# One level of Strassen's algorithm in the spatial product of a four-layer attention and gMLP kernel

## The chip, the cores and the metric

The kernel runs on one core of a Trainium2 chip. The metric is the device time of one execution in microseconds (us). The time before is the median of three runs.

## The reference

The input x has 2048 rows of 640 values. Four sublayers are added to it in turn: A, B, A, B, with the same weights in both rounds ("layer 1" and "layer 2" below; the code counts them 0 and 1).

A is an attention with memory: x is normalised, multiplied by wq, wk and wv, and treated in 4 segments of 512 rows and 32 heads of 20 columns. Each segment has a softmax attention within itself and a read from a memory matrix that the earlier segments have filled. The result goes through wo.

B is a gated product with mixing along the rows, and it is the part that the change touches:

```python
def _B_ref(x, w_in, w_sp, b_sp, w_out):
    z = _gelu(jnp.einsum("bsd,df->bsf", x, w_in))        # 640 -> 1728
    z1 = z[..., :Fh]                                     # Fh = 864
    z2 = _layernorm(z[..., Fh:], axis=-1)
    g = jnp.einsum("ts,bsf->btf", w_sp, z2) + b_sp[None, :, None]
    return jnp.einsum("bsf,fd->bsd", z1 * g, w_out)
```

The product of w_sp (2048 x 2048) with z2 (2048 x 864) is called the spatial product here.

## The kernel before, in words

The rows of x stand in 16 tiles of 128. All large products are made in 16-bit floats with a correction: each operand is split into a high and a low part (h, l), and three matmuls (h x h, h x l, l x h) take the place of one. Splitting takes one ScalarE operation (the scaled high part) and one VectorE operation (the rest). Where an operand must be turned, one DMA transpose from SBUF to SBUF turns both parts. All DMAs are issued from SyncE (SP), in one queue.

A layer has three stages, which follow one another in the code and overlap at their ends.

- **Attention (phase1a, L1195).** For each segment: normalised rows are split and turned into xt0 or xt1 (`prep`, L667), value products are made tile by tile (`value`, L686), query and key products in units of 128 columns (`unit`, L742), then logits, exponentials and their products with the values. The order of the matmuls is written out by hand: `run` (L1034) gives each piece of work a due time in steps, and streams named fills, background, dense and reads are merged by these times. `early` (L1041) does the first four tiles' rows and values and the first unit before the steps begin. The last results of a segment are cast and stored as ohl (L1022), in the same buffers (tag xh) that `prep` uses for its split rows. The weights wv, wq and wk are split once, in layer 1, and stay in SBUF for both layers (L177, L183).
- **phase1b (L302).** For each of the 16 tiles: the attention's output product (only tiles 12 to 15, the others had it in phase1a; `attn_out`, L331), normalisation of the row tile (xn), its split and transpose (`xn_t`: xnhl, then th), two half products with w_in of 30 matmuls of 432 columns each (`w_in_half`, L356), and the gelu. The second half gives z2: it is normalised and split into zh and zl, which stay in SBUF for all 16 tiles (`z2_half`, L367). The first half gives z1, which is stored (`z1_half`, L374). The weights of the second half (wi1) and wo are loaded during attention, those of the first half (wi0) near its end (L312).
- **phase2 (L400).** For each of the 16 tiles t: `rows(t)` loads 128 rows of w_sp, takes each row's largest value (L427), makes a power of two of it, splits the scaled rows in two halves of 1024 columns (L437, L438) and turns each half by a DMA transpose into wt (L439). `spatial(t)` makes 16 x 3 x 2 = 96 matmuls of 432 columns into one accumulator gp (L450), copies it with scale and bias (L453), multiplies with z1 (L455), takes the largest value of each row (L457), splits (L463, L464) and turns (L466) the result u into ut. `tail(t)` makes the output product with w_out, 42 matmuls (L479), adds x and stores the row tile (L482, L483). The loop issues spatial(t), rows(t+1), tail(t-1).

Buffers belong to pools; pools are laid out in SBUF one after another in the order in which they are opened, from the left end or (side="right") from the right end, and a stage's pools take over the addresses of the stage before. A new buffer waits only for the buffers of the old stage whose addresses it covers. Two padding tiles named gap (L309 in phase1b, 1945 words; L406 in phase2, 5580 words a partition) set which addresses meet. The order of the instructions on each engine other than the hand-written one is chosen when the kernel is built, by priority (the order in the code, raised by `high_priority`) and by when a modelled operand is ready.

## Time and profile before

| what | us |
|---|---|
| median of three runs | 2308.09 (2307.16 to 2308.31) |
| the profiled execution's own time | 2313.21 |
| its span from the first to the last instruction | 2311.5 |
| PE busy | 2167.8 |
| VectorE busy | 1372.8 |
| ScalarE busy | 1139.0 |
| GpSimd busy | 987.0 |

One execution of the kernel was recorded. In the profile, PE is TensorE's matmuls and PEld its weight loads, DVE is VectorE, ACT ScalarE, POOL GpSimd, SPq the queue of SyncE that issues the DMAs. A line such as `L450 PE MATMUL gp<-zh,wt` names the line of the kernel, the engine, the operation, the tile written and the tiles read; after it stand the shapes, the count, the busy time and the mean duration in ns, and then the idle time of the engine ahead of these instructions and what ended it. In a timeline the first number is the start in us, the second the length in us, and the brackets tell how long the engine had been idle and what ended that. The chain of waits follows the work that ended last back to the beginning; its lines give start, length, and what the time went to. The stages lie in the span as follows: attention to 613 us, phase1b to 813, phase2 to 1187, attention of layer 2 to 1731, phase1b to 1934, phase2 to the end; neighbouring stages overlap.

### The profile page before, as it was taken

The page shows a single profiled execution, that of the slowest core. Times are in us where ns is not written, and L with a number is a line of the kernel's source. Part 1 is how long each engine was busy: PE and PEld are TensorE (multiplying, and loading weights), DVE is VectorE, ACT ScalarE, POOL GpSimd, SP SyncE. Part 2 cuts the span into 40 slices and gives each one's busy share as a digit, 9 for nine tenths or more (in the row PEclk, how much of TensorE's full clock was granted, in tenths as well). Part 3 has the DMA queues.
Part 4 walks back from the last instruction along what each step waited for, and adds up shares of the span by engine and source line. Part 5 has one row for each costly group of instructions (what it writes and reads, how often), then busy time and mean ns, then how long its engine had stood idle before and what let it go on. Part 6 is the DMA issues. An engine that isn't in the chain of part 4 may idle for free.

```text
span 2311.5 us, 52604 instructions
## 1 busy us (share of the span) xinstructions
PE 2167.8 (94%) x21706; PEld 1306.2 (57%) x21706; DVE 1372.8 (59%) x2577; ACT 1139.0 (49%) x1344; POOL 987.0 (43%) x976
## 2 busy tenths in 40 slices
PE   5888889999899999999998989999989999999998
PEld 3455555666555555555554556566665555555554
DVE  7678878777754544343327786777756443534331
ACT  3578788888532322121126987888863322212110
POOL 2387889999610000000104988899991100000000
PEclk9999999999899999999999999999999999999999
DMA  5566665345743687566634465443565347756561
GB/s 167 148 159 157 169 165 133 84 119 133 212 127 86 150 231 158 160 156 162 148 86 107 113 149 144 124 102 106 139 172 127 94 118 201 164 155 163 154 147 47
DMA packets 512113, 325.60 MB, mean 141 GB/s; under 512 B 411488, under 2 KB 454368, under 8 KB 507520
## 3 DMA queue, kind: packets, MB, share of 16 engines
q1 hardware_dynamic: 511872, 322.23, 54.5%
q8 instruction: 170, 2.79, 0.5%
q14 instruction: 71, 0.58, 0.1%
HBM read 148.46 MB, written 85.61 MB: 101 GB/s over the span
## 4 chain that ended last, share of the span: by engine, by line
PE 56%; DMA 4%; POOL 4%; DVE 3%; ACT 3%; issue 2%; SPq 1%; DVEq 0%; ACTq 0%; POOLq 0%
PE gp L450 23%; PE zp L363 13%; PE cyp L479 8%; POOL PL L970 3%; PE qps L756 2%; PE pv L998 2%; PE vps L697 2%; PE kps L756 1%; PE mp L895 1%; DMA th<-xnhl 1%; PE yps L729 1%; PE yp L340 1%; ACT P L933 1%; PE es L895 1%; DVE mxs L959 1%
## 5 line engine op out<-in xcount | busy, mean ns | idle before, releaser
L970 POOL TENSOR_TENSOR PL<-P,PH 128x640 f16<-128x640 f32 x380 | 535.5, 1434 | 53.3 <-PE pv L998 43.6
L450 PE MATMUL gp<-zh,wt 128*128 128x432 f16 x2048 | 462.3, 346 | 0.0
L450 PEld LDWEIGHTS <-wt 128*128 128x128 f16 x3072 | 300.5, 98 | 257.6
L959 DVE TENSOR_REDUCE mxs<-mp 128x2 f32<-128x1024 f32 (+2 forms) x384 | 320.0, 861 | 140.5 <-PE mp L886 139.0
L933 ACT ACTIVATE P<-es,sc 128x1024 f32<-128x1024 f32 (+1 forms) x256 | 271.5, 1060 | 99.1 <-PE es L886 84.9
L465 POOL MEMSET un<- 128x64 f16 x32 | 5.0, 155 | 665.9 <-DMA ut<-un 632.7
L363 PEld LDWEIGHTS <-th 128*128 128x128 f16 x1920 | 188.6, 99 | 173.5 <-DMA th<-xnhl 9.7
L450 PE MATMUL gp<-zl,wt 128*128 128x432 f16 x1024 | 270.6, 346 | 0.0
L453 ACT ACTIVATE u<-gp,bsp,un 128x864 f32<-128x864 f32 x32 | 34.2, 1070 | 431.1 <-PE gp L450 419.6
L968 ACT CAST PH<-P 128x1280 f16<-128x1280 f32 x192 | 239.7, 1248 | 1.6
L272 POOL TENSOR_TENSOR lnrs<-lnve,mhalf 128x1 f32<-128x1 f32 x96 | 60.2, 635 | 421.2 <-DVE lnve L271 374.5
L427 DVE TENSOR_REDUCE am<-wr 128x1 f32<-128x2048 f32 x32 | 73.1, 2286 | 210.2 <-DMA wr<-in_B_w_sp_dram 210.2
L970 POOL TENSOR_TENSOR PL<-Pb,PH 128x640 f16<-128x640 f32 x124 | 177.1, 1454 | 12.4 <-PE pv L998 8.0
L697 PE MATMUL vps<-wvh,xt 128*128 128x320 f16 x640 | 156.6, 313 | 25.5 <-DVE relu L788 19.6
L479 PE MATMUL cyp<-wuh,ut 128*128 128x320 f16 (+1 forms) x896 | 165.1, 301 | 5.8 <-DMA ut<-un 5.8
L895 PEld LDWEIGHTS <-qk 64*128 64x128 f16 (+1 forms) x2048 | 78.2, 94 | 160.4 <-issue 140.0
L479 PEld LDWEIGHTS <-ut 128*128 128x128 f16 (+1 forms) x1344 | 132.1, 98 | 61.6 <-DMA ut<-un 6.6
L998 PE MATMUL pv<-vs,PL 128*128 128x41 f16 x2560 | 157.0, 181 | 4.7 <-POOL PL L970 4.3
L998 PE MATMUL pv<-vs,PH 128*128 128x41 f16 x2560 | 159.5, 182 | 1.1 <-DVE ab L1014 0.8
L363 PE MATMUL zp<-wi1h,th 128*128 128x432 f16 x640 | 151.2, 352 | 7.8 <-DMA th<-xnhl 7.6
L895 PE MATMUL es<-qk 64*128 64x512 f16 (+3 forms) x1024 | 124.8, 300 | 27.7 <-ACT P L933 20.1
L363 PE MATMUL zp<-wi0h,th 128*128 128x432 f16 x640 | 148.3, 346 | 0.0
(189 smaller groups left out, 4294.5 us busy)
## 6 DMA issues: line engine op xcount, KB each, us to landing
wr<-in_B_w_sp_dram SPq DMA_DIRECT2D x32, 1024.0 KB
qk<-st SPq DMA_DIRECT2D x256, 120.0 KB
z<-z SPq DMA_DIRECT2D x32, 432.0 KB
cz<-z SPq DMA_DIRECT2D x32, 432.0 KB
xt<-in_A_x_dram SPq DMA_DIRECT2D x32, 320.0 KB
st<-qhl SPq DMA_DIRECT2D x40, 256.0 KB
st<-khl SPq DMA_DIRECT2D x40, 256.0 KB
x<-x SPq DMA_DIRECT2D x32, 320.0 KB
```

What stands on the lines that cost most here:

```text
L363: nc.tensor.matmul(zp[:, n, :FHH], a[:, k, :], b[:, k, c:c + FHH], start=(k == 0 and j == 0), stop=(k == KD - 1 and j == 2))
L427: nc.vector.tensor_reduce(am, wr, AX.X, ALU.max, apply_absolute_value=True)
L450: nc.tensor.matmul(gp[:, n, :FHH], wt[:, k // 8, a, k % 8, :], b[:, k, n * FHH:(n + 1) * FHH], start=(k == 0 and j == 0), stop=(k == NT - ...
L479: nc.tensor.matmul(yp[:, n, :320], a[:kn[k], k, :], b[:kn[k], k, n * 320:(n + 1) * 320], start=(k == 0 and j == 0), stop=(k == KO - 1 and ...
L697: nc.tensor.matmul(ps, a[:, k, c], b[:, k, n * 320:(n + 1) * 320], start=(i == 0), stop=(i == 14))
L756: nc.tensor.matmul(ps, a[:, k, c], b[:, k, :], start=(i == 0), stop=(i == 14))
L895: nc.tensor.matmul(out[:, h, o:o + w], a[r, ac], b[r, bc], start=o == 0, stop=False, skip_group_check=True)
L933: g.exp = nc.scalar.activation(P, E, AF.Exp, scale=g.esc)
L959: e = nc.vector.tensor_reduce(mx[:, :, n, j], mp[:, :, o:o + w], AX.X, ALU.max)
L968: nc.scalar.copy(PH, P[:, h])
L970: (nc.gpsimd if h == 0 or n < self.N - self.TAIL else nc.vector).tensor_tensor(PL[:, c], P[:, h, c], PH[:, c], ALU.subtract)
L998: nc.tensor.matmul(pv[:, i, h, :], x[:, c:c + 128], v[:, j, h0 + h, :], start=(j == 0 and x is PH), stop=(j == i and x is PL), skip_group_ ...
```

## The change

The 16 tiles are paired as t and t + 8; the rows and columns of w_sp, and the rows and columns of z2, are thus cut into two halves each, so that the spatial product is a product of 2 x 2 blocks. It is made by one level of Strassen's algorithm (Winograd's form: four sums or differences of blocks for each operand): seven block products in place of eight.

- **phase1b** takes the tiles in the order 0, 8, 1, 9, ... and makes of each pair's z2 seven blocks of 432 columns (b11, b21, b22 of z2 itself, and four differences made on GpSimd), each split into zh and zl by ScalarE and VectorE. zh and zl grow from 16 x 864 to 8 x 7 x 432 columns each, 96.8 KB a partition in place of 55.3. The staging of w_in's first half uses the buffers of w_sp's rows. The padding goes.
- **phase2** works in 8 pairs. `rows(p)` loads both tiles' rows in two column parts, makes the same kind of sums and differences on w_sp (two on GpSimd, two on VectorE for each part), and splits and turns 14 blocks of 512 columns, into 17 buffers. The two tiles of a pair have scales of their own; their ratio, a power of two, enters the differences. The scales are kept from layer 1 for layer 2. `pair(p)` makes seven products of 8 x 3 matmuls of 432 columns into three accumulators, which ScalarE and VectorE read in between, and places the two tails of the pair before after the second and the fifth product. `finish` is the part of `spatial` after the copy.
- The query and key weights no longer stay in SBUF. In layer 1 they are stored to DRAM by 20 DMAs from the background stream of phase1a, at step 45, and in layer 2 they are loaded again by 4 DMAs. Their room is used by w_sp's rows and their split parts, and the start of zh, in phase1b and phase2. The pools for wo and wi1 change places.

The core of the diff:

```diff
-ZS = 1024.0
+ZS = 256.0
+WSP = 4096.0
...
-        for nm in "vqk":
-            g.w[nm] = [wp.tile([128, KD, D], F16, name=f"w{nm}{x}") for x in "hl"]
+        g.w["v"] = [wp.tile([128, KD, D], F16, name=f"wv{x}") for x in "hl"]
+        g.wqk = {nm + x: nc.dram_tensor(f"w_{nm}{x}", (128, KD, D), F16, kind="Internal").ap() for nm in "qk" for x in "hl"}
...
-        p2, p1, px1, gap = pool("b2", 2), pool("b1", 1), pool("bx1", 1), pool("bgap", 1)
+        p2, p3, px1 = pool("b2", 2), pool("b1", 3), pool("bx1", 1)
...
-        wi0 = g.wi[0].load(sp)
+        wi0 = g.wi[0].load(g.prep[0], 864, "wr")
...
+        def block(k, j, src):
+            nc.scalar.copy(zh[:, k, j, :], src)
+            nc.vector.tensor_tensor(zl[:, k, j, :], src, zh[:, k, j, :], ALU.subtract)
...
+            if t < 8:
+                b11, b12 = z[:, :FHH], z[:, FHH:]
+                block(k, 0, b11)
+                sub(b11, b12, b11)
+                block(k, 4, b11)
+                return
+            t1, b12 = z2[k][:, :FHH], z2[k][:, FHH:]
+            b21, b22 = z[:, :FHH], z[:, FHH:]
+            sub(t1, b22, t1)
+            block(k, 1, b21)
+            sub(b12, b12, b22)
+            block(k, 2, t1)
+            sub(b21, b21, t1)
+            block(k, 3, b12)
+            block(k, 5, b22)
+            block(k, 6, b21)
...
+WB = ("11", "12", "s2", "s3", "s1", "s4", "22")
...
+        def rows(p):
+            ws = []
+            for c in range(2):
+                w = pr.tile([128, S], F32, tag="wr", name="wr").rearrange("p (r h c) -> p r h c", r=2, h=2)
+                for r in range(2):
+                    t = p + 8 * r
+                    nc.sync.dma_start(w[:, r], w_sp[t * 128:(t + 1) * 128, :].rearrange("p (h c) -> p h c", h=2)[:, :, c * 512:(c + 1) * 512])
+                ws.append(w)
+            if not g.wsp_scaled:
...
+                def part(nm, src, r):
+                    hl = ph.tile([128, 2, 512], F16, tag="wn", name="wn")
+                    nc.scalar.activation(hl[:, 0], src, AF.Identity, scale=iv[r])
+                    nc.vector.scalar_tensor_tensor(hl[:, 1], src, iv[r], hl[:, 0], ALU.mult, ALU.subtract)
+                    t = blocks[nm, c] = pt.tile([128, 2, 4, 128], F16, tag="wt", name="wt")
+                    nc.sync.dma_start(t.rearrange("p l k c -> p (l k) c"), hl.rearrange("p l c -> p (l c)"), transpose=True)
+
+                part("11", a11, 0)
+                part("22", a22, 1)
+                nc.gpsimd.tensor_tensor(a22, a21, a22, ALU.add)
+                nc.vector.scalar_tensor_tensor(a21, a21, rho, a11, ALU.mult, ALU.subtract)
+                nc.vector.scalar_tensor_tensor(a11, a22, rho, a11, ALU.mult, ALU.subtract)
+                part("12", a12, 0)
+                part("s2", a11, 0)
+                nc.gpsimd.tensor_tensor(a12, a12, a11, ALU.subtract)
+                part("s3", a21, 0)
+                part("s1", a22, 1)
+                part("s4", a12, 0)
...
+        def product(ps, blocks, j, start):
+            for k in range(NP):
+                wt = blocks[WB[j], k // 4]
+                for i, (a, z) in enumerate(((0, zh), (0, zl), (1, zh))):
+                    nc.tensor.matmul(ps, wt[:, a, k % 4, :], z[:, k, ZB[j], :], start=start and k == 0 and i == 0,
+                                     stop=k == NP - 1 and i == 2, skip_group_check=True)
...
-            ut = p1.tile([128, 2, KO, 128], F16, tag="ut", name="ut")
+            ut = p2.tile([128, 2, KO, 128], F16, tag="ut", name="ut")
...
+            A = bank("ga")
+            product(A, blocks, 0, True)
+            copy(0, left)
+            C = bank("gc")
+            product(C, blocks, 1, True)
+            add(0, left, C)
+            if pend:
+                tail(*pend[0])
+            product(A, blocks, 2, False)
+            copy(1, left)
+            B = bank("gb")
+            product(B, blocks, 3, True)
+            product(A, blocks, 4, False)
+            copy(1, right)
+            add(1, right, B)
+            if pend:
+                tail(*pend[1])
+            product(A, blocks, 5, False)
+            copy(0, right)
+            f0 = finish(p, u[0])
+            product(B, blocks, 6, False)
+            add(1, left, B)
+            return f0, finish(p + 8, u[1])
...
+            if not g.wo.made:
+                for i, (nm, x, k) in enumerate((nm, x, k) for nm in "qk" for x in range(2) for k in range(KD)):
+                    with self.tc.issue_after(self.fetched.ins):
+                        self.nc.sync.dma_start(g.wqk[nm + "hl"[x]][:, k], g.w[nm][x][:, k])
+                    yield 45 + .05 * i
...
+                with tc.tile_pool(name="wqk", bufs=1, reuse_waits="tile") as qp:
+                    for nm in "qk":
+                        g.w[nm] = [qp.tile([128, KD, D], F16, name=f"w{nm}{x}") for x in "hl"]
+                        for hl, t in zip("hl", g.w[nm]):
+                            if layer:
+                                nc.sync.dma_start(t, g.wqk[nm + hl])
+                    phase1a(g, x, o_d, x1_d)
+                g.prep = [zs.enter_context(tc.tile_pool(name=n, bufs=b, reuse_waits="tile")) for n, b in (("cr", 2), ("ch", 3))]
...
-                zh = zp.tile([128, NT, FH], F16, name="zh")
-                zl = zp.tile([128, NT, FH], F16, name="zl")
+                zh = zp.tile([128, NT // 2, 7, FHH], F16, name="zh")
+                zl = zp.tile([128, NT // 2, 7, FHH], F16, name="zl")
```

More of the change, by code (lines that the diff above doesn't have):

```diff
@@ L302, in phase1b @@
 def phase1b(g, o_d, x, x1_d, z1_d, zh, zl):
+    ORDER = [t + 8 * r for t in range(NT // 2) for r in range(2)]
     nc, tc = g.nc, g.tc
@@ L447, in spatial @@
-            for k in range(NT):
-                for j, (a, b) in enumerate(((0, zh), (0, zl), (1, zh))):
-                    for n in range(2):
-                        nc.tensor.matmul(gp[:, n, :FHH], wt[:, k // 8, a, k % 8, :], b[:, k, n * FHH:(n + 1) * FHH],
-                                         start=(k == 0 and j == 0), stop=(k == NT - 1 and j == 2))
-            u = p1.tile([128, FH], F32, tag="u", name="u")
-            nc.scalar.activation(u.rearrange("p (n c) -> p n c", n=2), gp[:, :, :FHH], AF.Identity,
-                                 bias=bsp[:, t:t + 1], scale=un)
@@ L483, in tail, with pair, copy, add @@
             nc.sync.dma_start(out[t], xo.rearrange("p n c -> p (n c)"))
+        def pair(p, blocks, pend):
+            bank = lambda nm: pg.tile([128, 512], F32, tag=nm, name=nm)[:, :FHH]
+            un = [sc[:, 2, p, r:r + 1] for r in range(2)]
+            bias = [bsp[:, p + 8 * r:p + 8 * r + 1] for r in range(2)]
+            u = [p1.tile([128, FH], F32, tag=f"u{r}", name="u") for r in range(2)]
+            left, right = slice(0, FHH), slice(FHH, FH)
+            def copy(r, c):
+                nc.scalar.activation(u[r][:, c], A, AF.Identity, bias=bias[r], scale=un[r])
+            def add(r, c, ps):
+                nc.vector.scalar_tensor_tensor(u[r][:, c], ps, un[r], u[r][:, c], ALU.mult, ALU.add)
+            A = bank("ga")
[21 more added lines that the diff above has]
+            return f0, finish(p + 8, u[1])
         with tc.high_priority(offset=HP):
-            wt = rows(0)
-        wu = g.wu.load(sp, D)
+            blocks = rows(0)
+        wu = g.wu.load(p2, D, "xo")
         for _ in range(g.wu.nk + 1):
@@ L490, in phase2 @@
         pend = None
-        for t in range(NT):
-            if t == 5:
+        for p in range(NP):
+            if p == 2:
                 g.wu.keep()
-            u = spatial(t, wt)
-            wt = rows(t + 1) if t + 1 < NT else None
-            if pend is not None:
-                tail(*pend)
-            pend = (t, *u)
-        tail(*pend)
+            f = pair(p, blocks, pend)
+            blocks = rows(p + 1) if p + 1 < NP else None
+            pend = f
+        g.wsp_scaled = True
+        for f in pend:
+            tail(*f)
 def consts(g, ctx):
@@ L516, in consts @@
     g.sc = cp.tile([128, 11], F32, tag="sc", name="sc")
+    g.wsc = cp.tile([128, 4, NT // 2, 2], F32, tag="wsc", name="wsc")
+    g.wsp_scaled = False
     g.wap = cp.tile([128, 4, 10], F32, tag="wap", name="wap")
```

98 lines of the change are left out of this document (50 added, 48 removed).

## The prediction, made before the changed kernel was run

> **What bounds the kernel now.** I read the page's busy times first, then the busy times of each engine by stage (columns: stretch, its length, then busy us and instructions of PE, PEld, DVE, ACT, POOL, then granted clock, DMA share, GB/s), then the chain of waits.
>
> ```profile
> PE 2167.8 (94%) x21706; PEld 1306.2 (57%) x21706; DVE 1372.8 (59%) x2577; ACT 1139.0 (49%) x1344; POOL 987.0 (43%) x976
> 840.00:1175.00 335.00, 334.03 (x1992) 194.56 (x1991) 142.23 (x259) 60.82 (x59) 13.94 (x28) 1.00 0.64 159
> 1930.00:2290.00 360.00, 360.00 (x2127) 207.84 (x2125) 138.79 (x239) 61.66 (x58) 2.42 (x16) 1.00 0.61 152
> 1012.45 17.52 PE gp L450 x96
> 1029.97 5.71 PE cyp L479 x42
> ```
>
> The second and third lines are the two spatial stages (phase2): the matmul engine is busy for the whole stretch at full clock, everything else at most 64%. The chain is there nothing but 17.52 us of spatial product and 5.71 us of output product, tile after tile: 23.23 us a tile, 46.46 us for the two tiles t and t+8. So a matmul taken out of this stage comes out of the time, until another thing is late.
>
> **What is removed.** 96 matmuls of 432 columns take 17.52 us: 0.1825 us each. A pair of tiles takes 192 of them now; seven products of 8 x 3 are 168. One product is 24 x 0.1825 = 4.38 us, and one product fewer for 8 pairs in 2 layers is 16 x 4.38 = 70.1 us. Every matmul already has its own weight load (21706 of each), so smaller products add none. A pair should take 7 x 4.38 + 2 x 5.71 = 42.1 us.
>
> **What has to fit into 42.1 us.** The other engines' costs, by kind:
>
> ```profile
> L437 ACT ACTIVATE wn<-wr,ivw 128x1024 f16<-128x1024 f32 x64 | 73.0, 1147 | 128.4 <-DMA wt<-wn 112.3 <-DVE ivw L432 16.0
> L438 DVE SCALAR_TENSOR_TENSOR wn<-wr,ivw,wn 128x1024 f16<-128x1024 f32 x64 | 81.7, 1279 | 49.8 <-ACT wn L437 49.7
> L427 DVE TENSOR_REDUCE am<-wr 128x1 f32<-128x2048 f32 x32 | 73.1, 2286 | 210.2 <-DMA wr<-in_B_w_sp_dram 210.2
> L774 DVE SCALAR_TENSOR_TENSOR khl<-kps,khl 128x512 f16<-128x512 f32 x40 | 27.2, 681 | 13.7 <-ACT relu L773 13.7
> L794 DVE SCALAR_TENSOR_TENSOR phl<-relu,sc,phl 128x512 f16<-128x512 f32 x30 | 37.1, 1236 | 7.7 <-ACT phl L793 7.7
> L285 POOL TENSOR_TENSOR xnhl<-xt,xnhl 128x640 f16<-128x640 f32 x32 | 44.7, 1401 | 95.1 <-ACT xnhl L284 94.9
> 1006.70:1029.90 23.20, 23.20 (x140) 13.49 (x138) 10.02 (x17) 4.27 (x4) 0.15 (x1) 1.00 0.62 158
> ```
>
> VectorE now spends 10.0 us a tile (last line), 20.0 a pair, of which the four splits are 5.1 and the two reductions 4.6. The change makes 14 splits of 512 columns (0.68 each, L774's 681 ns: 9.5), four more such operations for the differences (2.7), three additions out of PSUM (some 0.6 each, an estimate from the same row: 1.8) and drops nothing else: 20.0 - 5.1 + 9.5 + 2.7 + 1.8 = 29 us of 42.1 in layer 1. In layer 2 the scales are kept, which takes off the 4.6: 24. ScalarE goes from 8.5 to some 12 by halves of L437's 1.15. GpSimd gets four operations of 512 columns, at most 1.4 us each by the 640-column row. None is the bound by its sum.
>
> DMA: 0.62 of 23.2 us is 14.4 us a tile, 28.8 a pair. The transposes grow from four of 512 KB to fourteen of 256 KB.
>
> ```profile
> 1030.00 4.65 SPq L439 DMA_TRANSPOSE wt<-wn  x2
> 1034.50 1.15 ACT L437 ACTIVATE wn<-wr,ivw 128x1024 f16<-128x1024 f32 x1 [3.42 <-DMA wt<-wn]
> 1036.77 1.15 ACT L437 ACTIVATE wn<-wr,ivw 128x1024 f16<-128x1024 f32 x1 [0.21 <-DMA wt<-wn]
> ```
>
> Two transposes go out at 1030.00; their buffers come free at 1034.50 and 1036.77, so the second costs 2.27 us. Fourteen halves are 15.9 us where four wholes were 9.1: 28.8 + 6.8 = 35.6 us of 42.1, 85%. That fits: of 17 wt buffers three are free for the next pair at once, each half product (2.2 us) leaves another, and a block is used about a pair later. I take nothing for it; it costs something when DMA takes over 1.18 times this price.
>
> **The output product of a pair's first tile.** Its u is complete only after the sixth product; its tail comes after the second product of the next pair, 3 x 4.38 = 13.1 us later. Now it has a whole tile.
>
> ```profile
> 1053.24 1.07 ACT L453 ACTIVATE u<-gp,bsp,un 128x864 f32<-128x864 f32 x1 [15.32 <-PE gp L450]
> 1061.41 1.30 SPq L466 DMA_TRANSPOSE ut<-un  x1
> 1066.65 0.15 POOL L465 MEMSET un<- 128x64 f16 x1 [24.25 <-DMA ut<-un]
> 2288.66 0.43 PE L479 MATMUL cyp<-wuh,ut 128*128 128x320 f16 x2
> 2299.37 0.71 PE L479 MATMUL cyp<-wuh,ut 128*128 128x320 f16 x2 [4.84 <-DMA ut<-un]
> 2299.37 8.03 PE cyp L479 x42
> ```
>
> From the end of a tile's products to the landing of its transpose: 13.4 us amid other work (1053.24 to 1066.65), 10.7 us at the end of the kernel, where nothing else runs (2288.66 to 2299.37). The new copy is half as wide (0.5 us less). So 10.2 to 12.9 against 13.1, with busier queues: a wait of 0 to 3 us for each of the 14 pairs that have a pair before them. I take 0.4 us, near the lower end because the sum still closes: **6 us** (0 to 41).
>
> **From layer 1's phase2 to layer 2's attention.** Until now padding tiles keep layer 2's first buffers (xt0, the x rows) off phase2's late ones, and the value products fill the waits:
>
> ```profile
> 1169.18 0.43 PE L479 MATMUL cyp<-wuh,ut 128*128 128x320 f16 x2
> 1174.89 0.30 PE L697 MATMUL vps<-wvh,xt 128*128 128x320 f16 x1
> 1181.17 5.71 PE cyp L479 x42
> 1196.90 0.59 PE L756 MATMUL qps<-xt,wqh 128*128 128x512 f16 x2
> ```
>
> 27.7 us from the last spatial matmul (1169.18) to the first query product, all full. The change takes the padding for the wider zh and zl. By the pools' sizes in order (per partition from the end of the value weights: 25.6 KB of query/key weights, then attention's pools) xt0 lies at 137 to 147 KB and the x rows at 147 to 152, where phase2 then has ut, x1 and w_out at 135 to 172. The first x row can be loaded only after the last tail's matmuls. Then: first tail at 10.2 - 4.4 = 5.9 us after the last product, 8.0 long at a half clock (2299.37 row), second tail 5.7: 19.6. Then load, statistics, scaling, split, transpose:
>
> ```profile
> 1735.68 2.78 DMA o<-ohl
> L269 DVE BATCH_NORM_STATS2 lnst<-xt 128x6 f32<-128x320 f32 x64 | 28.1, 477 | 13.7 <-DMA xt<-x 12.1 <-DMA xt<-in_A_x_dram 1.6
> L680 DVE TENSOR_SCALAR xt<-xt,lnmv,lnrs 128x640 f32<-128x640 f32 x32 | 28.3, 883 | 3.3 <-POOL lnrs L272 3.1
> L284 ACT CAST xnhl<-xt 128x640 f16<-128x640 f32 x32 | 23.1, 723 | 38.7 <-DVE xt L680 38.2 <-DVE mr L981 0.5
> 1747.84 3.36 DMA th<-xnhl
> ```
>
> 2.8 for the load (nearest transfer), some 2 for statistics and root (2 x 0.48 and the small ones), 0.9, 0.7, 1.4 (L285), 3.4: 11.2. Then 16.3 us of value products (27.7 less two tails of 5.71), plus 2.3 for a cold clock (8.03 against 5.71): 49.4 against 27.7, **+21.7 us**. Below: 16, if the row buffers are left by the first tail; above: 30, if the four rows come one by one.
>
> **From attention to phase1b, twice.** Now tiles 0 and 1 are normalised during attention and three half products are done before the first wait:
>
> ```profile
> 608.28 0.53 PE L363 MATMUL zp<-wi1h,th 128*128 128x432 f16 x2 [0.16 <-DVE xt L735]
> 613.44 0.18 PE L998 MATMUL pv<-vs,PL 128*128 128x41 f16 x1
> 614.19 0.89 PE L363 MATMUL zp<-wi1h,th 128*128 128x432 f16 x4
> 628.72 0.90 PE L363 MATMUL zp<-wi1h,th 128*128 128x432 f16 x2 [3.05 <-DMA th<-xnhl]
> 630.13 1.65 PE L363 MATMUL zp<-wi1h,th 128*128 128x432 f16 x4
> 1731.30 0.17 DVE L1009 TENSOR_TENSOR rs<-pv,iomg 128x8 f32<-128x8 f32 x1 [0.31 <-PE pv L998]
> L285 DVE TENSOR_TENSOR xnhl<-xn,xnhl 128x640 f16<-128x640 f32 x32 | 27.7, 866 | 10.1 <-ACT xnhl L284 10.0
> ```
>
> By the same addition xn and xnhl now lie at 152 to 157 KB, under attention's xh, which holds the last ohl until its store is read. That is 7.2 us after attention's last matmul (1731.30 to 1735.68 + 2.78); scaling, cast, difference and transpose take 6 more (0.9 by L680, 0.7, 0.9, 3.4 and signals). So the first half product starts 13.2 us after attention instead of 5 us before its end. By 628.72 three halves of 5.5 us were done; then one has run for 2 us: 14 behind, less the 4.4 us by which those matmuls and w_in's splits held attention up: 10. In layer 2, where the start was already held up, I take 8. Together **+18 us** (8 to 30; the upper end if w_in's first half, now under Pb, is late too).
>
> The row after the 3.05 us wait shows a half clock: 1.65 us for four matmuls instead of 0.89. The Trainium skill, TensorE: Matmul & The Clock Gate, section "Why this matters for your kernels", says the same against this change: no idle gaps over some 3 us between bursts. By that page's 3.4 us window at half rate each gap costs 1.7 us, not the 2.3 taken here; over four new gaps my sum would be 2 us lower.
>
> **Smaller terms.** Twenty stores of query/key weights in one step of layer 1's attention: ten loads of w_in in layer 2 now hold SP 0.43 us each (the second of them, below), and an x row queued behind them came late:
>
> ```profile
> 1705.01 0.43 SPq L106 DMA_DIRECT2D wi0l<-w_i0l  x1
> 1715.67 0.55 DVE L735 SCALAR_TENSOR_TENSOR xt<-yps,sc,xt 128x320 f32<-128x320 f32 x1 [2.46 <-DMA xt<-x]
> ```
>
> That held VectorE for 2.5 us; 20 issues, 8.6 us of SP with fetches of qk and maxima queued behind, I put at **4 us** (0 to 10). The loads in layer 2 run during the last pair; the last one waits for zh and has 5 us of the gap above. Phase1b's three extra blocks a pair (at most 0.7 us each on VectorE by L774, 0.6 on ScalarE by half of L437) lie beside 21.9 us of matmuls (120 of 0.1825): **3 us** over both layers (0 to 16) for later th. Pair order itself costs nothing: x rows 0 to 3 are written first as before. The end: 1 us, the first tail's wait.
>
> **Sum.** -70.1 + 6 + 21.7 + 18 + 4 + 3 + 1 = -16.4. The profiled execution took 2313.2 us (span 2311.5), 5.1 above the median of 2308.1; its after is 2297, the median's **2292**.
>
> **Rivals.** (1) *The output product waits for ut in every pair.* Place: the tail after the second product. It decides from 13.1 us of chain on; at 14.7 us (1.6 x 14 = 22) the gain is gone; at 16 us it costs 41 instead of 6: +19, 2327. For it: 13.4 us measured now, amid less work; against it: the new pieces are shorter. (2) *The hand-overs are mostly hidden*, because buffers come free earlier than the addition says: 6 instead of 40 left: 2258. Against it: the first-row and ohl waits are plain. (3) *VectorE and GpSimd hold each other up.* 512 columns from SBUF take 1.236 us in attention, beside a busy GpSimd, where 1024 take 1.279 in phase2 beside an idle one. At 1.236 the 18 such operations take 22 us instead of 12, VectorE 39 of 42.1: the chain of (1) grows some 1.2 us a pair: 17 us, 2309. The Trainium skill, SBUF — State Buffer, section "Who interferes with whom", has this rule for two-input VectorE instructions beside GpSimd reads; the two rows agree with it. (4) *Phase2 keeps its old pace* because 14 transposes cost over 1.18 times the price above: no 70 us, only losses: +54, 2362.
>
> **Chances.** Forecast 0.54, of which 0.05 ends within 0.2% of before; (1) 0.17, slower; (2) 0.16, faster; (3) 0.09, of which 0.07 the same; (4) 0.04. 0.2%, 4.6 us, is what a measurement can tell here. Faster 0.49 + 0.16 = 0.65; same 0.12; slower 0.17 + 0.02 + 0.04 = 0.23. The forecast's own terms reach from 2275 to 2306; with the middle of (1) and (2) the range is 2258 to 2328.
>
> **What would show it.** Right: pairs of 42 to 43 us in phase2, VectorE 65 to 70% and DMA 80 to 90% there; 15 us or more without matmuls between the layers and some 13 after each attention, each followed by a half clock. Wrong: waits of PE for ut of over 1.6 us a pair, waits for wt, or value products between the last tails.

## The result, and the profile after

The changed kernel takes 2430.38 us (median of four runs, 2425.49 to 2438.13) against 2308.06 for the kernel before: a ratio of 1.0534, 95% interval 1.0506 to 1.0562. It is 122 us slower where 16 us of gain were forecast. The profiled execution took 2438.1 us (span 2436.1).

First the page of the changed kernel: busy times, and the shares of the chain of waits by engine and by line. The last row is the chain of the kernel before, by engine.

```profile
PE 2151.3 (88%) x21322; PEld 1281.4 (53%) x21322; DVE 1577.1 (65%) x2825; ACT 1262.2 (52%) x1616; POOL 1147.4 (47%) x1104
PE 33%; DMA 8%; DVE 6%; ACT 4%; issue 3%; POOL 3%; SPq 1%; ACTq 0%; DVEq 0%; POOLq 0%
PE zp L364 7%; PE ga L504 6%; PE cyp L533 5%; DMA wt<-wn 4%; PE gb L504 3%; POOL PL L1063 2%; PE pv L1091 2%; PE qps L849 1%; PE vps L790 1%; PE kps L849 1%; PE mp L988 1%; DMA ut<-un 1%; DMA wr<-in_B_w_sp_dram 1%; DVE wn L483 1%; ACT P L1026 1%
PE 56%; DMA 4%; POOL 4%; DVE 3%; ACT 3%; issue 2%; SPq 1%; DVEq 0%; ACTq 0%; POOLq 0%
```

TensorE has 384 matmuls fewer, as intended, but is busy for only 16.5 us less (2151.3 against 2167.8): the mean granted clock of the profiled execution fell from 0.986 to 0.956. The chain runs less through products (33% of the span for 56%) and more through DMA (8% for 4%); the transposes into wt are now 4% of it. Now three pairs of layer 2's phase2, busy times by engine (columns as in the prediction: stretch, length, PE, PEld, DVE, ACT, POOL, granted clock, DMA share, GB/s).

```profile
2097.00:2149.00 52.00, 43.66 (x250) 24.63 (x248) 29.17 (x46) 17.53 (x25) 7.84 (x8) 0.97 1.04 214
2197.70:2242.50 44.80, 42.23 (x253) 24.41 (x252) 23.70 (x39) 13.58 (x19) 5.22 (x5) 1.00 0.87 192
2242.50:2292.00 49.50, 45.18 (x253) 25.51 (x254) 24.81 (x40) 15.89 (x22) 5.53 (x7) 0.93 0.87 187
```

And what TensorE and ScalarE waited for in that stage (total, times, longest):

```profile
PE ga L504 <- ACT u L547: 25.3, 13, 5.3
ACT wn L482 <- DMA wt<-wn: 175.8, 79, 7.8
```

A pair takes 45 to 52 us where 42.1 were forecast and 46.5 were taken before. TensorE's largest wait is for ScalarE's copy of an accumulator (L547); in layer 1's phase2 it is 19.7 us. In the kernel before, TensorE's waits in phase2 come to 1.0 us in layer 1 and to none in layer 2 before the last tile. VectorE's 24 to 29 us a pair stand beside a forecast of 24; in three stretches of some 50 us of layer 1 it is busy for 30 to 34, beside 29. In the second and third row no engine is full by its sum; in the first the DMA engines are (1.04). What holds the copy is seen in the timeline: the last matmul of one product into ga and the first of the next on TensorE, then ScalarE's instructions in order.

```profile
2131.26 0.35 PE L504 MATMUL ga<-zh,wt 128*128 128x432 f16 x1
2145.45 0.52 PE L504 MATMUL ga<-zh,wt 128*128 128x432 f16 x1 [5.28 <-ACT u L547]
...
2126.32 0.69 ACT L547 ACTIVATE u<-ga,bsp,wsc 128x432 f32<-128x432 f32 x1
2132.79 0.72 ACT L482 ACTIVATE wn<-wr,wsc 128x512 f16<-128x512 f32 x1 [5.78 <-DMA wt<-wn]
2133.78 1.51 ACT L482 ACTIVATE wn<-wr,wsc 128x512 f16<-128x512 f32 x2 [0.26 <-DMA wt<-wn]
2137.81 0.72 ACT L482 ACTIVATE wn<-wr,wsc 128x512 f16<-128x512 f32 x1 [2.52 <-DMA wt<-wn]
2141.47 1.01 ACT L518 ACTIVATE un<-u,uivw 128x864 f16<-128x864 f32 x1 [2.94 <-DVE uivw L515]
2143.16 0.72 ACT L482 ACTIVATE wn<-wr,wsc 128x512 f16<-128x512 f32 x1 [0.68 <-DMA wt<-wn]
2144.08 0.72 ACT L482 ACTIVATE wn<-wr,wsc 128x512 f16<-128x512 f32 x1 [0.20 <-DMA wt<-wn]
2144.71 0.69 ACT L547 ACTIVATE u<-ga,bsp,wsc 128x432 f32<-128x432 f32 x1
```

The product into ga ends at 2131.6. Its copy, 0.69 us long, starts at 2144.71: in ScalarE's order six splits of the next pair's w_sp and one cast of u stand ahead of it, and all but one of these wait, for a transpose to leave a buffer or for VectorE. TensorE fills 8 of these 13 us with products into the other banks and then stands. (The Trainium skill, Perfetto Trace Analysis, section "Tensor Engine Instruction (MATMUL, LD_WEIGHTS)", notes that ScalarE, VectorE and GpSimd work strictly first in, first out; these rows agree.)

Where the time went, stage by stage, by the two timelines:

| stretch | before | after | change | forecast |
|---|---|---|---|---|
| layer 1 to the end of attention's products | 613.6 | 623.1 | +9.5 | +4 |
| from there to the first half product, layers 1 and 2 | -5.3, -0.2 | 21.8, 17.3 | +44.6 | +18 |
| phase1b to the first block product, both | 194.0, 191.8 | 194.5, 188.7 | -2.6 | +3 |
| phase2 to the last block product, both | 367.0, 365.9 | 389.3, 384.6 | +41.0 | -64.1 |
| last block product to layer 2's first query product | 27.6 | 54.8 | +27.2 | +21.7 |
| layer 2's attention | 534.4 | 538.2 | +3.8 | 0 |
| last block product to the end | 22.7 | 23.7 | +1.0 | +1 |

105 of the 141 us between forecast and profile lie in phase2. They have two parts. Up to the first tail, a layer's first pair should take 39.5 us (nine products) and 5.5 for a half product of phase1b that runs among them. It took 62.6 and 68.2, together 41 too many. In the timeline of the changed kernel, the first three splits in layer 1, the first transposes, the first product and the first tail:

```profile
663.70 1.94 ACT L482 ACTIVATE wn<-wr,wsc 128x512 f16<-128x512 f32 x3
830.06 10.81 SPq L485 DMA_TRANSPOSE wt<-wn  x5
839.43 0.35 PE L504 MATMUL ga<-zh,wt 128*128 128x432 f16 x1
902.01 0.67 PE L533 MATMUL cyp<-wuh,ut 128*128 128x320 f16 x2 [0.56 <-DMA ut<-un]
```

And in that of the kernel before, the first transposes and the first product:

```profile
776.84 6.11 SPq L439 DMA_TRANSPOSE wt<-wn  x2
802.32 0.53 PE L450 MATMUL gp<-zh,wt 128*128 128x432 f16 x2
```

Before, the first transposes went out 25 us ahead of the first product. Now three parts have been split since 666 us, and the first transpose goes out at 830, 9 us ahead. The other 64 us are the later pairs: from the first tail to the last product 642 us in the two layers. The two hand-overs are of the kind that the prediction described. First TensorE's waits between the layers, then, in the timeline, the last block product and the first query product, and the way from attention's last product to the first half product in layer 2:

```profile
PE vps L790 <- DMA xt<-xnhl: 14.2, 1, 14.2
PE cyp L533 <- DMA ut<-un: 8.2, 1, 8.2
```

```profile
1228.38 0.35 PE L504 MATMUL gb<-zh,wt 128*128 128x432 f16 x1
1283.49 0.59 PE L849 MATMUL qps<-xt,wqh 128*128 128x512 f16 x2
1821.54 0.20 PE L1091 MATMUL pv<-vs,PL 128*128 128x41 f16 x1
1839.06 0.90 PE L364 MATMUL zp<-wi1h,th 128*128 128x432 f16 x2 [17.32 <-DMA th<-xnhl]
```

### The profile page after: what moved, and what is told of

Read it like the earlier page. It is cut to its first block, busy times and chain, and to the rows that moved or that the text cites. A ratio compares the mean times of both kernels' runs of the same rounds, so it can differ in the third digit from the quotient of the medians.

```text
span 2436.1 us, 53187 instructions
## 1 busy us (share of the span) xinstructions
PE 2151.3 (88%) x21322; PEld 1281.4 (53%) x21322; DVE 1577.1 (65%) x2825; ACT 1262.2 (52%) x1616; POOL 1147.4 (47%) x1104
## 4 chain that ended last, share of the span: by engine, by line
PE 33%; DMA 8%; DVE 6%; ACT 4%; issue 3%; POOL 3%; SPq 1%; ACTq 0%; DVEq 0%; POOLq 0%
PE zp L364 7%; PE ga L504 6%; PE cyp L533 5%; DMA wt<-wn 4%; PE gb L504 3%; POOL PL L1063 2%; PE pv L1091 2%; PE qps L849 1%; PE vps L790 1%; PE kps L849 1%; PE mp L988 1%; DMA ut<-un 1%; DMA wr<-in_B_w_sp_dram 1%; DVE wn L483 1%; ACT P L1026 1%
## 5 line engine op out<-in xcount | busy, mean ns | idle before, releaser
L504 PEld LDWEIGHTS <-wt 128*128 128x128 f16 x2688 | 267.8, 100 | 313.6 <-issue 81.6
L504 PE MATMUL ga<-zh,wt 128*128 128x432 f16 x1024 | 293.8, 358 | 46.6 <-ACT u L547 45.0
L482 ACT ACTIVATE wn<-wr,wsc 128x512 f16<-128x512 f32 x224 | 157.7, 718 | 313.7 <-DMA wt<-wn 261.7
L483 DVE SCALAR_TENSOR_TENSOR wn<-wr,wsc,wn 128x512 f16<-128x512 f32 x224 | 181.5, 822 | 182.4 <-ACT wn L482 181.2
L489 POOL TENSOR_TENSOR wr<-wr 128x512 f32<-128x512 f32 x32 | 44.3, 1385 | 334.9 <-DVE wn L483 286.9
L790 PE MATMUL vps<-wvh,xt 128*128 128x320 f16 x640 | 161.5, 320 | 38.0 <-DVE relu L881 19.6
L533 PE MATMUL cyp<-wuh,ut 128*128 128x320 f16 (+1 forms) x896 | 171.7, 308 | 24.6 <-DMA ut<-un 24.6
L1063 POOL TENSOR_TENSOR PL<-Pb,PH 128x640 f16<-128x640 f32 x124 | 176.3, 1448 | 19.1 <-PE pv L1091 16.7
L504 PE MATMUL ga<-zl,wt 128*128 128x432 f16 x512 | 183.6, 359 | 0.0
L1091 PE MATMUL pv<-vs,PL 128*128 128x41 f16 x2560 | 158.2, 182 | 11.2 <-POOL PL L1063 7.0
L504 PE MATMUL gb<-zh,wt 128*128 128x432 f16 x512 | 145.8, 353 | 14.0 <-DMA wt<-wn 7.1
```

The lines of the kernel that those rows point to most:

```text
L482: nc.scalar.activation(hl[:, 0], src, AF.Identity, scale=iv[r])
L483: nc.vector.scalar_tensor_tensor(hl[:, 1], src, iv[r], hl[:, 0], ALU.mult, ALU.subtract)
L504: nc.tensor.matmul(ps, wt[:, a, k % 4, :], z[:, k, ZB[j], :], start=start and k == 0 and i == 0, stop=k == NP - 1 and i == 2, skip_group_c ...
L533: nc.tensor.matmul(yp[:, n, :320], a[:kn[k], k, :], b[:kn[k], k, n * 320:(n + 1) * 320], start=(k == 0 and j == 0), stop=(k == KO - 1 and ...
L790: nc.tensor.matmul(ps, a[:, k, c], b[:, k, n * 320:(n + 1) * 320], start=(i == 0), stop=(i == 14))
L1063: (nc.gpsimd if h == 0 or n < self.N - self.TAIL else nc.vector).tensor_tensor(PL[:, c], P[:, h, c], PH[:, c], ALU.subtract)
```

## The experiments

Every ratio is to the kernel before on the same chip, with its interval; the change itself is at 1.0534. The theories have letters in the expectations. The main ones: A, the three buffers wn; B, DMA engines that are full; C, the 17 buffers wt; D, the order on ScalarE; E, addresses at the hand-overs; H, VectorE's reductions that wait for loads.

**More buffers, another order, and the price of transposes.** More wn buffers (from a pool of its own behind w_out):

```diff
+        ph2, made = pool("ch2", 2), [0]
...
-                    hl = ph.tile([128, 2, 512], F16, tag="wn", name="wn")
+                    q = ph2 if p and made[0] % 5 > 2 else ph
+                    made[0] += 1
+                    hl = q.tile([128, 2, 512], F16, tag="wn", name="wn")
```

> Change: two more buffers for the split parts (wn) in phase2, five in place of three, all else as in the changed kernel. Theory A (the three wn buffers: ScalarE stands at a split until a transpose has read a buffer, and the copy of an accumulator is queued behind that split, so TensorE waits for the copy): pairs fall from 48 us to 43 or 44, the whole to 2350-2375. Theory B (the DMA engines are full, 14 transposes of 256 KB cost nearly what wholes cost): pairs stay at 47-49, the whole within 10 us of 2430. Theory C (transposes stand in the queue for one of the 17 turned buffers wt, and hold what is behind them): within 10 us of 2430.

Measured 1.054 (1.0504 to 1.0575), 2433.2 us: no difference. ScalarE waits less for a wn, TensorE as long for the copy:

```profile
ACT wn L485 <- DMA wt<-wn: 126.5, 62, 7.9
PE ga L507 <- ACT u L550: 24.3, 12, 4.3
```

Theory A falls as far as the number of buffers goes; its other half, the copy behind a blocked split, is theory D. The same bytes for wt, `NWT = 19`:

> Change: the same bytes spent on two more buffers for turned blocks (wt), 19 in place of 17. Theory C: the 33 us in which transposes stood in the queue until TensorE left a wt go, the whole falls by 40 us or more, to 2390 or less. Theories A and B: within 10 us of 2430.

Measured 1.0646 (1.0615 to 1.0677), 2457.6: 27 us slower. In its profile phase1b is 18 us longer over the two layers and phase2 some 8, so C's 40 us are nowhere and C falls; why more room costs time was not followed up. The order alone:

```diff
+                    n = len(blocks)
+                    with ExitStack() as b:
+                        if copies:
+                            b.enter_context(tc.issue_after(copies[0 if n < 4 else 1 if n < 7 else 2 if n < 10 else 3].ins))
-                    nc.scalar.activation(hl[:, 0], src, AF.Identity, scale=iv[r])
+                        nc.scalar.activation(hl[:, 0], src, AF.Identity, scale=iv[r])
```

> Change: the same buffers, but in ScalarE's order the splits of the next pair stand behind given accumulator copies: the first four behind the first copy, three behind the second, three behind the third, the rest behind the fourth. Theory A: what hurts is the copy behind a blocked split, so fewer splits ahead of each copy win back part of it: 2380-2410. Theory B: within 10 us of 2430. Theory C: within 10 us, since the transposes go out in the same order.

Measured 1.0424 (1.039 to 1.0458), 2406.5: 25 us won with the same buffers, loads and transposes, within the 2380 to 2410 of theory A's other half. In layer 2 the wait for the copy has gone from 25.3 to 3.0 us, and phase2 is 20 us shorter. In layer 1 the wait stays (19.1 us for 19.7) and phase2 is 3 us shorter: there the order of the splits alone wins next to nothing. The row is layer 2's:

```profile
PE ga L509 <- ACT u L553: 3.0, 2, 2.2
```

The transposes by themselves, in a kernel that does nothing else:

> Not the kernel: only transposes from SBUF to SBUF, in six sections one after another, each read by ScalarE as it lands: 8 of 512 KB, 16 of 256 KB, 16 of 256 KB with four loads of 512 KB between them in runs of 2 KB, the same with runs of 4 KB, and 16 of 256 KB from split parts through a ring of three buffers and of five. It computes nothing of the reference. Forecast's price: 2.27 us for 512 KB, 1.135 for 256 KB. Theory B: 1.7 us or more for 256 KB with nothing beside it, and rings of three and five equally fast. Theory A: 1.1 to 1.3 us for 256 KB alone, the ring of three 2 us or more a part, the ring of five under 1.5.

The rows of its timeline are ScalarE's reads of what has landed: the first and the last of 8 of 512 KB, the first and the last of 16 of 256 KB, then the first and the last of four loads in 2-KB runs, each behind four of 256 KB.

```profile
14.46 0.20 ACT L30 CAST mark<-d 128x16 f32<-128x16 f16 x1 [4.55 <-DMA d<-src]
31.74 0.20 ACT L30 CAST mark<-d 128x16 f32<-128x16 f16 x1 [2.20 <-DMA d<-src]
36.53 0.20 ACT L30 CAST mark<-d 128x16 f32<-128x16 f16 x1 [2.31 <-DMA d<-src]
57.17 0.20 ACT L30 CAST mark<-d 128x16 f32<-128x16 f16 x1 [1.04 <-DMA d<-src]
68.94 0.19 ACT L65 COPY mark<-wr 128x1 f32<-128x1 f32 x1 [2.64 <-DMA wr<-in_B_w_sp_dram]
90.42 0.19 ACT L65 COPY mark<-wr 128x1 f32<-128x1 f32 x1 [2.21 <-DMA wr<-in_B_w_sp_dram]
```

The window over the 16, with the DMA share next to last:

```profile
34.50:57.10 22.60, 0.00 (x0) 3.05 (x15) 0.00 (x0) 1.00 0.97 186
```

512 KB take (31.74 - 14.46) / 7 = 2.47 us, 256 KB (57.17 - 36.53) / 15 = 1.38: half the size costs 56%. Four of them and a load of 512 KB take (90.42 - 68.94) / 3 = 7.16 us, the load 7.16 - 4 x 1.38 = 1.6 of it. Fourteen are 19.3 us, not the forecast's 15.9. That is dearer, but 3.4 us a pair only, and less than the 1.7 us for 256 KB that theory B asked for. (The Trainium skill, DMA: Bandwidth & Descriptors, section "Latency and other measured facts", has 261 GB/s for a transpose with a non-contiguous middle dimension, measured in one kernel, and some 350 to 400 for the contiguous case. By the lower figure 512 KB would take 2.0 us, an estimate. Measured here were 212 GB/s and, for 256 KB, 190.)

**DMA load against order.** Loads left out (`n = 16 if c in held else 512` columns of each block):

> Left out: after the first pair of each layer, w_sp's rows are not loaded (16 columns of each block stand for the 512), so that the sums are made of stale rows; the splits, differences, transposes and matmuls are all made. It takes 2 MB of 6.7 MB off the DMA engines in each pair. Theory B (DMA near full: transposes and loads queue behind one another, so splits, copies and ut come late): pairs of layer 2 fall from 47.2 us on average to 42-43.5, the whole to 2360 or less. Theory D (order only: a copy queued behind a blocked split, whatever the load): pairs stay over 46, the whole over 2410.

```profile
2166.60:2262.70 96.10, 87.57 (x505) 50.03 (x503) 48.26 (x78) 28.96 (x40) 10.57 (x11) 0.96 0.70 143
2262.72:2351.47 88.75, 83.75 (x488) 48.23 (x488) 42.30 (x68) 24.76 (x33) 8.34 (x11) 0.96 0.66 138
```

Measured 1.0428 (1.0407 to 1.0449), 2408.6. Each row is two pairs: with the DMA engines at 0.66 to 0.70 a pair still takes 44 to 48 us. B gave 2360 or less; it falls as the main cause, though 24 us show that load has a share in it. Theory D's bounds (every pair over 46 us, the whole over 2410) are not quite met either. Then the order of pools, two lines:

```diff
-        p2, p3, px1 = pool("b2", 2), pool("b1", 3), pool("bx1", 1)
+        p2, px1 = pool("b2", 2), pool("bx1", 1)
         pe2, pe3, pe1 = pool("be2", 2), pool("be3", 3), pool("be1", 1)
+        p3 = pool("b1", 3)
...
-        p1, p2, wp = pool("c1", 1), pool("c2", 2), pool("cw", 1)
+        wp, p1, pz, p2 = pool("cw", 1), pool("c1", 1), pool("cz", 2), pool("c2", 2)
```

> Change: only the order in which pools are opened. phase1b puts x1, th, xn and xnhl where attention had xt1 and xt0, and z2 where it had the xh buffers of ohl; phase2 puts w_out first, and u, un and z1 where layer 2's attention has xt0 and its x rows, ut and x1 behind them. Theory E (addresses: new buffers wait for the late readers of the old ones): from the last block product to the first query product 27-37 us in place of 55; from attention's last product to the first half product of phase1b under 10 us in place of 20 and 22; the whole to 2375-2400. Theory F (the queue and the work before are late anyway, the addresses matter little): these three gaps shrink by less than 5 us each, the whole stays over 2415.

Measured 1.0446 (1.0425 to 1.0467), 2412.7. At the starts of phase1b theory E holds: the first half product follows attention's last product at once, at 620.9 and 1817.3, 39 us won in the two. The profile shows 25 in all (the medians 18), since layer 1's phase2 (9 us) and layer 2's attention (5) became longer. Between the layers it falls: 56.4 us. SyncE's order shows why:

```profile
1236.06 6.05 SPq L538 DMA_DIRECT2D x<-xo  x2
1242.20 0.88 SPq L766 DMA_DIRECT2D xt<-x  x2
```

Layer 2's first rows are issued behind the two last result stores, which wait for the last tails. Next, the stores of query and key weights alone, added to the kernel before:

> The kernel before with one part of the change alone: the query and key weights are stored by 20 DMAs at the same place, and loaded again in layer 2 into the same buffers. Theory G (20 stores in one place stop the queue for layer 1's attention): attention of layer 1 ends 8 to 13 us later, 2316 to 2322. The forecast's term: +4 us, 2310 to 2314.

Measured 1.0032 (1.002 to 1.0045), 2316.8: 7 us (5 to 10), at the lower edge of theory G and above the forecast's 4. In its profile layer 1's attention ends 4.8 us later, as the forecast has it and not the 8 to 13 of theory G.

**The split on another engine, no maxima, three edits together.** The high part by `nc.gpsimd.tensor_scalar`:

> Change: the high part of each split of w_sp is made by GpSimd instead of ScalarE; buffers, transposes, loads and sums stay. ScalarE then has only the accumulator copies and the casts of u in phase2. Theory D (a copy that frees an accumulator stands on ScalarE behind splits that wait for transposes): TensorE's waits for the copy, 25 us in layer 2's phase2 and 13 in layer 1's, fall to under 5 each, and the whole to 2370-2405. Rival (the splits come late on whichever engine makes them, and TensorE would wait for the turned blocks instead): waits for wt take their place, the whole stays over 2420, or rises if GpSimd takes over 1.2 us a split.

The group of the high parts on GpSimd (busy, mean ns, idle before it), and TensorE's waits in layer 2's phase2:

```profile
L482 POOL TENSOR_SCALAR wn<-wr,wsc 128x512 f16<-128x512 f32 x105 | 180.0, 1720 | 98.3 <-DMA wt<-wn 66.2 <-DVE pw L448 8.2 <-DVE wr L491 6.4
```

```profile
PE ga L504 <- DMA wt<-wn: 11.8, 5, 7.3
PE ga L504 <- ACT u L547: 6.0, 4, 3.5
```

Measured 1.0649 (1.0617 to 1.0682), 2459.6. The wait for the copy falls from 25.3 to 6.0 us in layer 2, and from 19.7 to 5.6 in layer 1, near what theory D said. But the splits come late at 1.72 us each: TensorE's waits for wt grow from 8.1 to 22.6 us in layer 2 and from 7.4 to 30.5 in layer 1, and those for ut in layer 1 from 9.3 to 32.8. Phase2 is 8 us shorter in layer 2 and 38 longer in layer 1. The rival holds. Without the row maxima (`nc.vector.memset(pw, 2.0 ** -9)`, on the run with ordered splits):

> The ordered splits of the earlier run, and in place of the row maxima of w_sp in layer 1 one fixed scale (2 to the power -9) for all rows, so that 32 reductions of 1024 columns and their waits for loads are left out; layer 2 unchanged. Theory H (VectorE stands in its order at reductions that wait for loads, 45 us in layer 1, and the additions of accumulators and the steps to ut are behind them): layer 1's pairs fall from about 50 us to 44-46, the whole 25 to 45 us under the run with ordered splits (2406): 2361-2381. Rival (layer 1 is slow for other reasons): within 10 us of 2406.

First a reduction of the run with ordered splits, with its wait; then, without the maxima, two pairs of layer 1 and four of layer 2:

```profile
956.25 1.22 DVE L466 TENSOR_REDUCE am<-wr 128x1 f32<-128x1024 f32 x1 [8.13 <-DMA wr<-in_B_w_sp_dram]
```

```profile
1069.91:1153.16 83.25, 83.25 (x500) 48.75 (x501) 45.76 (x75) 26.45 (x38) 10.49 (x12) 1.00 0.88 187
2051.88:2144.41 92.53, 86.87 (x508) 50.09 (x506) 50.61 (x82) 28.31 (x42) 12.98 (x12) 0.98 0.97 209
2230.84:2314.51 83.67, 83.42 (x500) 48.71 (x500) 45.69 (x75) 26.46 (x38) 10.49 (x12) 1.00 0.87 186
```

Measured 1.0278 (1.0225 to 1.033), 2373.7: 33 us more, as theory H said; 25 of them are in layer 1's phase2 and 6 in layer 1's phase1b. In layer 1 the wait for the copy falls from 19.1 to 5.1 us. With the maxima ScalarE's splits stood 33.5 us there for VectorE's sums and 20.1 for the scales, without them 9.8 and 4.1. The edit also takes 32 reductions of 1.22 us off VectorE, so what their waits cost and what their work costs is not told apart. In the first row a pair takes 83.25 / 2 = 41.6 us, TensorE busy throughout at full clock, DMA at 0.88. Of the five stretches of two pairs, four have 41.6 to 43.2 us a pair at a DMA share of 0.87 to 0.96; the fifth, right behind layer 2's first tail (second row), has 46.3 at 0.97. So the forecast's 42.1 us can be had with all 14 transposes and all loads, once the copies and additions come in time.

The ordered splits, the order of pools, and the last two stores on ScalarE's queue:

> Three edits together: the ordered splits, the new order of pools, and the last pair's two result stores of each layer issued from ScalarE's queue instead of SyncE's, so that layer 2's first x rows do not stand behind them. If the first two add up: 2407 - 18 = 2389. Theory I (between the layers, the x rows were issued behind the last two stores, which wait for the last tails): the gap from the last block product to the first query product falls from 56 to 35-40 us, the whole to 2370-2378. Rival (the rows wait for addresses after all): the gap stays over 50, the whole at 2385-2395.

Measured 1.0328 (1.0298 to 1.0358), 2385.5: the first two add up, theory I does not hold. The first x rows were issued at 1227.7 us instead of 1242.2, but the gap is still 51.7 us, as the rival said, but for these first rows not for its reason, addresses. On VectorE their statistics stand behind the last tail's result:

```profile
1234.58 0.89 DVE L542 SCALAR_TENSOR_TENSOR xo<-cyp,xs,cx 128x640 f32<-128x640 f32 x1 [4.82 <-PE cyp L539]
1235.38 1.27 DVE L270 BATCH_NORM_STATS2 lnst<-xt 128x6 f32<-128x320 f32 x3
```

**The first pair, and the sum of the edits.** Alternating column parts, `for it in (its * 7 if p == 0 else [its[0]] * 7 + [its[1]] * 7): next(it)`:

> The ordered splits of the earlier run, and for the first pair of each layer alone the two column parts are turned alternately, so that the first product can end after the second transpose instead of the eighth, and the second after the sixth instead of the tenth. Theory J (the first pair goes at the pace of its transposes in their order): from the first block product to the first tail, 62.7 and 70.9 us in the run with ordered splits, falls by 6 to 15 us in each layer, the whole from 2406 to 2378-2395. Rival (the first pair is late because its transposes start late and everything else is loaded at once, in whatever order): within 5 us of these, the whole within 8 us of 2406.

Measured 1.044 (1.0415 to 1.0466), 2406.9: nothing, the rival. The first product no longer waits inside, but the first tail comes 65.6 and 66.4 us after it: TensorE now waits 8.9 us for a later block in layer 1's first pair and 9.2 for a copy in layer 2's. All of it together:

> All edits that won something, together: ordered splits, the fixed scale in place of the row maxima (as in the earlier run with it), phase1b's pools in the new order (phase2's as in the change), the first pair's column parts alternately, and the 20 stores spread, one every two steps, from step 70 on. If the parts add up: 2374, less 41 for the two starts of phase1b, less 7 for the stores, less 10 to 20 for the first pairs: 2306-2316, about the kernel before. Rival (what is won at one place is given back at the next queue, as the new order of pools gave 18 of its 41 us): 2325-2350.

Measured 1.021 (1.0184 to 1.0235), 2352.7: the rival, 2.7 us over its upper end. In layer 2's first pair a copy now stands behind a split whose rows are still being loaded, behind 14 loads of w_out (the next expectation says 12):

```profile
2002.43 0.72 ACT L484 ACTIVATE wn<-wr,wsc 128x512 f16<-128x512 f32 x1 [12.50 <-DMA wr<-in_B_w_sp_dram]
2003.06 0.69 ACT L560 ACTIVATE u<-ga,bsp,wsc 128x432 f32<-128x432 f32 x1
```

So the loads of these rows were put first (`nxt = loads(1)` ahead of w_out's), without and with the maxima:

> The sum of edits of the run before (2353), with one more: the loads of the second pair's w_sp rows are issued ahead of the 12 loads (layer 1: with their splits) of w_out, so that ScalarE's next split does not stand at a load while the accumulator copies are queued behind it (9.3 us once in layer 2's first pair, 8.3 in layer 1's). Theory K (the first pair is late by what is queued on SyncE between its transposes and the next rows): from the first block product to the first tail, 70.9 and 67.2 us, falls by 6 to 12 in each layer, the whole to 2330-2342. Rival (w_out then comes late, or the stall moves to the next wait): over 2346.

> The same with the row maxima of w_sp computed again as in the change, so that nothing is left out. If what the maxima cost was measured rightly by the run without them (33 us against the run with ordered splits): 33 us over the other run, 2363-2375 by theory K. If they are hidden once the rows come earlier: under 10 us over it.

Measured 1.0152 (1.0101 to 1.0202), 2344.5, and 1.0244 (1.0186 to 1.0302), 2365.9. The first time lies between theory K and its rival, but theory K's mechanism falls: the first tail comes later, after 78.3 and 76.1 us, and the later pairs are 24 us shorter in all. In layer 1's first pair TensorE stands 16.0 us for one copy; on ScalarE, splits that wait for loads of w_sp and w_out and for a transpose are ahead of it. The maxima cost 21 us here, not 33. Last, phase1b's pairs in the order 0, 4, 5, 6, 7, 1, 2, 3:

> The run with ordered splits and the first pair's column parts alternately (2407), and phase1b takes the pairs in the order 0, 4, 5, 6, 7, 1, 2, 3, so that the last output product with wo (tile 15) is at the tenth tile instead of the last; 6 of the 17 buffers wt lie on wo's addresses. Theory L (the first pair's transposes have had their split rows ready for 160 us and wait for addresses of wo and wi1): the first transposes go out some 60 us before phase2 instead of 10, the first product no longer waits, and the time from the first block product to the first tail, 65.6 and 66.4 us, falls by 8 to 15 in each layer; the whole to 2378-2393. Rival (six early blocks do not help, since ScalarE's copies stand behind loads and splits in the first pair all the same): within 8 us of 2407.

> The sum of all edits with the earlier loads of the second pair's rows (2344, fixed scale in place of the row maxima), and the same new order of pairs in phase1b. Theory L: 2315-2330. Rival: within 8 us of 2344.

Measured 1.0401 (1.0343 to 1.0459), 2399.4, and 1.016 (1.011 to 1.021), 2343.9: theory L falls. wo is left earlier, but the first transposes still go out 9 us ahead of the first product (at 824.1 us). On SyncE they stand behind a store of z1, as in the changed kernel (a store at 829.69 us, the transposes at 830.06), and SyncE waits up to 9.6 us for the z of such a store:

```profile
814.34 0.32 SPq L400 DMA_DIRECT2D z<-z  x1
814.70 11.37 SPq L490 DMA_TRANSPOSE wt<-wn  x5
```

Why the build puts them there stays open. No version beat the kernel before; the best, at 1.0152, has a fixed scale.

## Why the prediction was wrong

- **The step that failed** is in "What has to fit into 42.1 us": "None is the bound by its sum", and "That fits ... I take nothing for it". The sums were near (VectorE in layer 2 24 to 29 us for 24, in layer 1 30 to 34 for 29; DMA, forecast 35.6 us of 42.1, took 0.88 x 41.6 = 36.6 in the clean pairs above and up to 0.96 x 42.6 = 41 in others). What they leave out is the order. The change made TensorE depend, four times a pair, on a copy within one or two products, and put that copy into a queue with 14 splits that wait for transposes. Before, one copy a tile had a whole tile's time, with two buffers gp. The prediction read the release of wn's buffers as the price of a transpose only, and priced no queue on ScalarE. The run with ordered splits and without maxima shows the size: its later pairs take 584 us for 642, so 58 of the 64 us that they were over the forecast are gone, with the transposes and loads unchanged. In layer 2 the order of the splits did it (316 to 293 us), in layer 1 the missing maxima (324 to 292; order alone 326 to 324). The second of these also leaves out work, so in layer 1 the cause is in part argued. The first pairs became 9 us longer, so that phase2 as a whole won 49 of its 105 us back.
- **The first pair** had no term at all. "A block is used about a pair later" does not hold for it: 41 us in the changed kernel. The rows show late transposes, and copies behind waiting splits when the transposes come in a better order. The DMA engines are nearly full there (shares of 0.93 and 1.02 in the two first pairs), which no run took away. From the first half product of phase1b to the first tail it is 257 us in each layer, and no run made that more than some 8 us shorter; so the cause of these 41 us stays open.
- **The price of transposes** was mis-sized: 1.135 us of 256 KB for 1.38 measured, 3.4 us a pair. With w_sp's loads left out 24 us came back, so DMA has a part; that it has it by making each wait in the queue longer is argued, not shown.
- **Rival (4)**, phase2 at its old pace (2362, 0.04), came nearest, but its reason is not the main one. Its condition is met as written, 1.38 us being 1.21 times the price, and still pairs of 41.6 to 43.2 us were had with all 14 transposes. **Rival (1)**: waits for ut were 9.3 us in layer 1's phase2 and, but for the last tail, 1.2 in layer 2's: 0.75 a pair for 0.4 forecast, small beside the rest. **Rival (2)** falls, the hand-overs cost more, not less. **Rival (3)** falls: a split took VectorE 0.82 us for the 0.68 of the forecast, not 1.24, and its sums stayed under the rival's 39 us.
- **Between the layers** the mechanism was right and the size near: +27.2 for +21.7 (upper end 30). The wait for ut was 8.2 for 5.9, the first rows' chain 14.2 for 11.2. The reason given, addresses, is not the only one: with other addresses the rows stood behind stores on SyncE, and then behind results on VectorE.
- **From attention to phase1b**: the mechanism was right (the new order of pools brought both gaps to zero), the size was not: 44.6 us for 18. The estimate of 13.2 us from attention's end became 17.3 in layer 2; and from 21.8 in layer 1 not 4.4 but nothing came back in attention, which ended 9.5 us later (4.8 with the stores alone).
- **The 20 stores**: +4 (0 to 10) forecast, 7 (5 to 10) measured by themselves. **The removed product** is as forecast: 41.6 us a pair where nothing else is late.
- The predicted signs: DMA at 80 to 90% came roughly true (0.82 to 1.04 in the stretches of phase2), VectorE's 65 to 70% only in layer 1 (61 to 67%, in layer 2 49 to 56%), and idle time followed by a half clock did (two matmuls took 0.90 us behind the gap of 17.3, where two take 0.53 at full clock). "Pairs of 42 to 43 us" did not. Of the signs of being wrong, waits for wt came, 7 to 8 us in each layer's phase2. The sign that was missing from the list is the one that decided, a wait of TensorE for ScalarE.

## What to carry to other kernels

When a change makes an engine that is never full read an accumulator that the next product needs, its busy sum does not tell when it will read it: list what stands ahead of that read in its queue, and what each of those waits for. A wait that is moved by one edit (another engine, more buffers, an earlier load) came back here, again and again, at the next in-order queue, so ask for each edit what is queued behind the wait that remains. More buffers did not help here; the order of the same instructions did, in layer 2.

## What the runs showed of the hardware

- In the kernel of transposes alone, those from SBUF to SBUF took 2.47 us for 512 KB and 1.38 for 256 KB, one after another, with the DMA share at 0.97 to 1.09. A 512-KB load among them added 1.6 us in runs of 2 KB and 1.5 in runs of 4 KB.
- Through a ring of three buffers (ScalarE, VectorE, transpose) a 256-KB part took 1.57 us, through five 1.38: with nothing beside it the ring was no limit at a pair's pace of 3.0 us a part, and not the 2 us or more that theory A asked for.
- GpSimd took 1.72 us for a scaled 512-column cast that takes ScalarE 0.72, and VectorE's second half of the split beside it 1.1 us instead of 0.82.
